# Reordering block 0 of a fused RWKV-6 and tanh-shrink kernel: decays ahead of the feed-forward part on VectorE in three steps, totals and first decays of block 1 in the boot, level 1 in step 0

## Chip, cores, metric

One core of one Trainium2 chip. The metric is the device time of one execution in microseconds (us). The program runs on one core only; the record gives the state of every run used here as fast. Runs of the kernel before still differ by up to 0.7% (those of one experiment by 1.1%), which matters for a change of this size; what the traces show of the reason stands at the end.

## The reference, cut

```python
# RWKV-6 attention, (batch, heads, seq, head_dim) = (4, 8, 768, 48)
for t in range(S):
    cur = np.einsum('bhd,bhe->bhde', u[None] * kt, vt)
    y[:, :, t] = np.einsum('bhd,bhde->bhe', rt, state + cur)
    state = wt[:, :, :, None] * state + np.einsum('bhd,bhe->bhde', kt, vt)
# then, on x = y as (3072, 384):
h = x @ w_in              # (384, 2048)
g = h - np.tanh(h)
return (g @ w_out).astype(np.float32)
```

Attention and feed-forward arithmetic are fp32; the two weight matrices arrive as 64-bit floats and are converted on the chip.

## The kernel before

The 3072 tokens are cut into 8 blocks of 384. Attention of a block is a doubling scheme over chunks of 64 tokens: at each level m = 1, 2, 4, 8, 16, 32 TensorE makes a gram matrix of r and k, VectorE or ScalarE copies the masked part of it out, and VectorE multiplies ("decays") half of k (`kq`) and half of r (`rp`) by products of w ("totals"), in place, for the next level. After that come a transpose ("turn"), the state update and the result.

Only block 0's attention runs alone, in the "boot". From then on, while the feed-forward part of block i runs in 16 steps f = 0 to 15, the attention of block i+1 is slotted between them. The listing sets the order on each engine, and no scheduler changes it later (`manual_schedule`). The trace shows VectorE keep to it: decay 2, listed behind the products of step 1, starts behind them at 60.40 us, though it could have begun at 56.7.

```python
def level(self, ps, m, p0, n, put_off=None):
    ...                                       # m == 32 has a variant of its own
    gr = self.gram(ps, self.tiles["kq"], self.tiles["rp"], p0, n, m, L // 2)   # TensorE
    ins = self.decay(m, p0, n)                # VectorE: kq, rp *= totals, after the gram has read them
    ...                                       # copies of the gram: VectorE for m <= 8, else ScalarE

def first(xT, f, ps):                         # feed-forward, step f
    hp = ps.tile([P, NB], F32, name="hp", tag="hp")
    for kc in reversed(range(KC)):            # 3 fp32 matmuls
        nc.tensor.matmul(hp, lhsT=w_in_sb[:, f, kc, :], rhs=xT[:, kc, :], ...)
    ...                                       # 6 activations on ScalarE: h, s, qa, qb, th, big
    return g, [ ... ], made                   # 5 products on VectorE, run later as "rest"

def plan(i):
    names = ("level 1", 2, 4, 8, 16, 32, "turn", "update", "result")
    if i == 0:
        steps = (1, 2, 3, 4, 6, 8, 10, 11, 13)                 # the step of each name
        before, behind = {0: ("totals 1", "kq", "rp")}, {1: ("totals 2",)}
        converted = (1, 3, 3, 4, 5, 7, 10, 10, 12, 13)         # steps of weight conversions 6 to 15
        loads = {f: "weights" for f in (1, 2, 3, 4, 6, 7, 8, 9, 10)}
    ...

for f in range(NF):                           # main loop of block i
    g, next_rest, made = first(here, f, ps_d)
    waiting.append((second, f, g))
    for n, op in enumerate(rest):             # products of step f - 1, mixed with the
        op()                                  # VectorE half of a weight conversion ("extra")
        if n >= 2 and extra:
            extra.pop(0)()
    for op in extra:
        op()
    rest = next_rest
    if later:
        for name in before.get(f, ()):
            later.prepare(name)               # totals, first decays
        if f in phases:
            later.phase(ps_a, phases[f])      # a level, turn, update or result of block i + 1
        ...
    for _ in range(converted.count(f)):
        extra += convert(*raws.pop(0))        # ScalarE half now, VectorE half in step f + 1
    if len(waiting) > LAG:                    # second matmul, three steps behind
        s, fs, gs = waiting.pop(0)
        s.add(fs, gs)
```

In what follows, hp5 is the first feed-forward matmul group of step 5, acc2 the second one of step 2 (TensorE runs it at the end of step 5), gram 8 the gram of level 8, decay 4 the pair of decays that level 4 makes, and gT the products' result that acc reads. In the traces each matmul of the listing shows as two, so a group of three is "x6".

## Time and profile before

| | before |
|---|---|
| median time, first three runs | 673.23 us (672.33 to 675.09) |
| span of the profiled run | 670.6 us |
| TensorE busy / granted clock over the span | 96% / 0.985 |
| VectorE, ScalarE busy | 81%, 73% |
| block 0 from hp0 to block 1's first hp | 84.6 us, of which 71.6 us is work at full clock |

"Busy" on TensorE says that an instruction was in flight, not that it ran at full clock (from 62.4 to 68.5 us it is busy for 6.10 of 6.10 us at a granted clock of 0.54), so busy share and granted clock are read together. The prediction shows the page, the stretches and TensorE's timeline. Its flips are changes of TensorE's granted clock between 0.50 and 1.00, its 952 is the time in ns of one decay (128x768, fp32), and its 400 is what the DMA engines moved, in GB/s (401 from 46 to 48 us, 412 from 48 to 50). What it tells in words only is the order on VectorE. This is VectorE's timeline of the kernel before (start, length, line, operation, output and inputs, shape), from the products of step 1 to decay 2:

```profile
56.72 0.55 DVE L488 SCALAR_TENSOR_TENSOR hs<-h,s 128x384 f32<-128x384 f32 x1
...
59.06 0.95 DVE L175 CUSTOM_DVE_ANT_0 w_sb<-w_sb,up 128x1536 uint16<-128x1536 uint16 x1
59.93 0.58 DVE L496 COPY_PREDICATED gT<-big,th 128x384 f32<-128x384 int32 x1
60.40 0.94 DVE L274 TENSOR_TENSOR kq<-kq,tot 128x768 f32<-128x768 f32 x1
61.27 0.95 DVE L274 TENSOR_TENSOR rp<-rp,tot 128x768 f32<-128x768 f32 x1
```

The two decays (the last two lines) could have begun at 56.7, when gram 2 had read what they overwrite, but 3.7 us of products and a conversion stand ahead of them. Gram 4 starts right after the last line has ended (62.36).

### The profile page before, as it was taken

The page shows a single profiled execution, that of the slowest core. Times are in us where ns is not written, and L with a number is a line of the kernel's source. Part 1 is how long each engine was busy: PE and PEld are TensorE (multiplying, and loading weights), DVE is VectorE, ACT ScalarE, POOL GpSimd, SP SyncE. Part 2 cuts the span into 40 slices and gives each one's busy share as a digit, 9 for nine tenths or more (in the row PEclk, how much of TensorE's full clock was granted, in tenths as well). Part 3 has the DMA queues.
Part 4 walks back from the last instruction along what each step waited for, and adds up shares of the span by engine and source line. Part 5 has one row for each costly group of instructions (what it writes and reads, how often), then busy time and mean ns, then how long its engine had stood idle before and what let it go on. Part 6 is the DMA issues. An engine that isn't in the chain of part 4 may idle for free.

```text
span 670.6 us, 19961 instructions
## 1 busy us (share of the span) xinstructions
PE 643.4 (96%) x8480; PEld 413.0 (62%) x8480; DVE 545.1 (81%) x1101; ACT 489.0 (73%) x966; POOL 5.0 (1%) x19
## 2 busy tenths in 40 slices
PE   4867999999999999999999999999999999999998
PEld 4745666566665666656665666656666566655554
DVE  7779998799778997599975998679976899746664
ACT  4678799775868667785776758677677857768785
POOL 2000000000000000000000000000000000000000
PEclk9968999999999999999999999999999999999999
DMA  8754354423112313121311231113131200000000
GB/s 316 224 209 149 103 177 137 151 72 97 50 55 58 112 49 96 58 70 50 96 49 57 72 95 51 52 53 120 50 95 38 91 3 2 2 11 35 1 0 36
DMA packets 30841, 54.37 MB, mean 81 GB/s; under 512 B 2336, under 2 KB 28704, under 8 KB 30752
## 3 DMA queue, kind: packets, MB, share of 16 engines
q1 hardware_dynamic: 30336, 52.80, 24.3%
q8 instruction: 67, 1.10, 0.7%
q10 hardware_dynamic: 352, 0.25, 0.1%
q14 instruction: 22, 0.18, 0.1%
q0 software_dynamic: 64, 0.05, 0.0%
HBM read 47.19 MB, written 4.72 MB: 77 GB/s over the span
## 4 chain that ended last, share of the span: by engine, by line
PE 76%; DVE 8%; issue 4%; PEld 4%; ACT 4%; DMA 2%; PEldq 1%; SPq 0%; DVEq 0%; ACTq 0%
PE acc L509 33%; PE hp L471 30%; PE att L242 8%; DVE states L371 2%; PE att L409 2%; PEld att L391 2%; PEld hp L471 2%; PE att L342 2%; PEld acc L509 1%; PE att L319 1%; DMA kq<-in_kT 1%; DVE rp L274 1%; DVE w_sb L175 1%; DVE hs L488 1%; DMA raw<-in_weights 1%
## 5 line engine op out<-in xcount | busy, mean ns | idle before, releaser
L471 PE MATMUL hp<-xT,w_sb 128*128 128x384 f32 x768 | 272.6, 492 | 3.0 <-ACT xT L423 2.1
L509 PE MATMUL acc<-w_sb,gT 128*128 128x384 f32 x768 | 275.2, 495 | 0.0
L471 PEld LDWEIGHTS hp<-xT,w_sb 128*128 128x128 f32 x768 | 147.2, 192 | 106.6 <-issue 2.4
L509 PEld LDWEIGHTS acc<-w_sb,gT 128*128 128x128 f32 x768 | 141.2, 191 | 89.5 <-ACT o L514 2.3
L478 ACT ACTIVATE h<-hp 128x384 f32<-128x384 f32 x128 | 62.9, 491 | 143.2 <-PE hp L471 142.5
L493 DVE TENSOR_TENSOR th<-h,th 128x384 f32<-128x384 f32 x128 | 70.9, 554 | 46.9 <-ACT th L482 46.8
L488 DVE SCALAR_TENSOR_TENSOR hs<-h,s 128x384 f32<-128x384 f32 x128 | 71.0, 554 | 27.2 <-ACT s L479 27.2
L496 DVE COPY_PREDICATED gT<-big,th 128x384 f32<-128x384 int32 x128 | 76.1, 595 | 12.8 <-ACT h L478 0.5
L480 ACT ACTIVATE qa<-s,shift 128x384 f32<-128x384 f32 x128 | 78.8, 615 | 4.2
L488 DVE SCALAR_TENSOR_TENSOR gT<-qb,hs 128x384 f32<-128x384 f32 x128 | 71.4, 558 | 9.2
L483 ACT ACTIVATE big<-s,shift 128x384 f32<-128x384 f32 x128 | 76.8, 600 | 0.0
L481 ACT ACTIVATE qb<-s,shift 128x384 f32<-128x384 f32 x128 | 76.8, 600 | 0.0
L488 DVE SCALAR_TENSOR_TENSOR hs<-qa,hs 128x384 f32<-128x384 f32 x128 | 70.5, 551 | 0.0
L479 ACT ACTIVATE s<-h 128x384 f32<-128x384 f32 x128 | 67.0, 523 | 4.0
L242 PEld LDWEIGHTS att<-rp,kq 48*64 48x64 f32 x3072 | 54.4, 148 | 22.5 <-issue 15.5
L482 ACT ACTIVATE th<-h 128x384 f32<-128x384 f32 x128 | 64.9, 507 | 0.0
L242 PE MATMUL att<-rp,kq 48*64 48x32 f32 x3072 | 58.3, 231 | 6.3 <-DVE rp L274 5.8
L274 DVE TENSOR_TENSOR kq<-kq,tot 128x768 f32<-128x768 f32 (+1 forms) x45 | 38.6, 857 | 2.8 <-PE att L319 1.6
L274 DVE TENSOR_TENSOR rp<-rp,tot 128x768 f32<-128x768 f32 (+1 forms) x45 | 38.8, 861 | 0.0
L371 DVE SCALAR_TENSOR_TENSOR states<-states,tot,att 128x48 f32<-128x48 f32 x176 | 31.5, 256 | 8.9 <-PE att L360 8.9
L302 DVE COPY_PREDICATED scores<-mask_all,att 128x384 f32<-128x384 uint8 (+1 forms) x54 | 31.8, 654 | 0.0
L242 PE MATMUL att<-rmix,kmix 48*64 48x64 f32 x768 | 14.5, 232 | 6.8 <-ACT rmix L222 6.8
(54 smaller groups left out, 336.4 us busy)
## 6 DMA issues: line engine op xcount, KB each, us to landing
raw<-in_weights SPq DMA_DIRECT2D x16, 768.0 KB, 4.4
rmix<-in_rT SPq DMA_DIRECT2D x7, 768.0 KB, 4.8
kmix<-in_kT SPq DMA_DIRECT2D x7, 768.0 KB, 4.8
wt<-in_wT SPq DMA_DIRECT2D x7, 768.0 KB, 4.7
kq<-in_kT SPq DMA_DIRECT2D x7, 768.0 KB, 5.2
rp<-in_rT SPq DMA_DIRECT2D x7, 768.0 KB, 4.6
v_sb<-in_v SPq DMA_DIRECT2D x8, 576.0 KB, 4.2
out_y<-o SPq DMA_DIRECT2D x23, 192.0 KB, 1.9
```

What stands on the lines that cost most here:

```text
L242: nc.tensor.matmul(dst, lhsT=lhs[rows, t0:t0 + L], rhs=src, start=True, stop=True)
L274: ins = nc.vector.tensor_tensor(out=part, in0=part, in1=by, op=ALU.mult)
L471: nc.tensor.matmul(hp, lhsT=w_in_sb[:, f, kc, :], rhs=xT[:, kc, :], start=(kc == KC - 1), stop=(kc == 0))
L479: nc.scalar.activation(out=s, in_=h, func=AF.Square)
L480: nc.scalar.activation(out=qa, in_=s, func=AF.Square, bias=shift[:, 0:1])
L481: nc.scalar.activation(out=qb, in_=s, func=AF.Square, bias=shift[:, 1:2])
L482: nc.scalar.activation(out=th, in_=h, func=AF.Tanh)
L483: nc.scalar.activation(out=big, in_=s, func=AF.Relu, bias=shift[:, 2:3])
L488: return lambda: nc.vector.scalar_tensor_tensor(out=out, in0=in0, scalar=scalar, in1=in1, op0=op0, op1=ALU.mult)
L493: lambda: nc.vector.tensor_tensor(out=th, in0=h, in1=th, op=ALU.subtract),
L496: lambda: nc.vector.copy_predicated(out=g, mask=big.bitcast(I32), data=th)], made
L509: nc.tensor.matmul(acc, lhsT=g[:, j * P:(j + 1) * P], rhs=w_out_sb[:, f, :], start=(f == 0), stop=(f == NF - 1))
```

## The change

The intent is to keep TensorE fed in block 0. It has four parts: work moved into the boot; earlier steps for each level; in steps 4 to 6 ("urgent") the level's VectorE work listed ahead of the products; and, not named in the title, later steps for most weight conversions.

```diff
         if i == 0:
-            steps = (1, 2, 3, 4, 6, 8, 10, 11, 13)
-            before, behind = {0: ("totals 1", "kq", "rp")}, {1: ("totals 2",)}
-            converted = (1, 3, 3, 4, 5, 7, 10, 10, 12, 13)
-            loads = {f: "weights" for f in (1, 2, 3, 4, 6, 7, 8, 9, 10)}
+            steps = (0, 2, 4, 5, 6, 7, 9, 10, 12)
+            before, behind, urgent = {}, {}, (4, 5, 6)
+            converted = (3, 4, 5, 5, 7, 9, 9, 10, 11, 13)
+            loads = {f: "weights" for f in (0, 1, 2, 3, 4, 6, 7, 8, 9, 10)}
 ...
@@ boot, after the loads of kq and rp
-        more_weights(nc.sync)
-        for _ in range(2):
-            ready.append(convert(*raws.pop(0)))
         while ready:
             converted()
+        for name in ("totals 1", "totals 2"):
+            later.prepare(name)
+        for name in ("kq", "rp"):
+            ready.append(convert(*raws.pop(0)))
+            converted()
+            later.prepare(name)
 ...
@@ main loop; finish() runs the products and conversions, as before
-            (products and conversions)
+            if f not in urgent:
+                finish(rest, extra)
             if later:
                 (prepare, phase)
+            if f in urgent:
+                finish(rest, extra)
```

More of the change, by code (lines that the diff above doesn't have):

```diff
@@ L530, in plan @@
             before = {0: ("kmix",), 1: ("rmix",), 2: ("totals 1",), 3: ("totals 2", "kq"), 4: ("rp",)}
-            behind, converted = {}, ()
+            behind, converted, urgent = {}, (), ()
             loads = {2: "v", 5: "rmix", 7: "kmix", 9: "wt", 11: "kq", 14: "rp"}
-        return dict(zip(steps, names)), before, behind, converted, loads
+        return dict(zip(steps, names)), before, behind, converted, loads, urgent
     blocks = [Block(b, q) for b in range(B) for q in range(NQ)]
@@ L625, with finish @@
     waiting, rest, extra = [], [], []
+    def finish(rest, extra):
+        for n, op in enumerate(rest):
+            op()
+            if n >= 2 and extra:
+                extra.pop(0)()
+        for op in extra:
+            op()
     for i, blk in enumerate(blocks):
@@ L631 @@
             xT = later.begin()
-        phases, before, behind, converted, loads = plan(i)
+        phases, before, behind, converted, loads, urgent = plan(i)
         second = Second(blk.b * S + blk.q * NB, ps_d)
@@ L636 @@
             waiting.append((second, f, g))
-            for n, op in enumerate(rest):
-                op()
-                if n >= 2 and extra:
-                    extra.pop(0)()
-            for op in extra:
-                op()
-            rest = next_rest
+            if f not in urgent:
+                finish(rest, extra)
             if later:
@@ L651 @@
                     later.prepare(name)
+            if f in urgent:
+                finish(rest, extra)
+            rest = next_rest
             name, ins = loads.get(f), None
```

## The prediction

> **What bounds the kernel now.** I read the page first (busy shares and the slices), then the engines in long stretches, then TensorE and VectorE in order of time through block 0, then the DMA landings. The page:
>
> ```profile
> PE 643.4 (96%) x8480; PEld 413.0 (62%) x8480; DVE 545.1 (81%) x1101; ACT 489.0 (73%) x966; POOL 5.0 (1%) x19
> ...
> PE   4867999999999999999999999999999999999998
> ...
> PEclk9968999999999999999999999999999999999999
> ```
>
> TensorE is full from the fifth slice to the end; a change of order can only win in the first four (to about 67 us) or in what they hand on. The stretches of block 0, from its first feed-forward matmul (42.5) to the first of block 1 (127.1):
>
> ```profile
> 42.50:51.00 8.50, 7.53 (x11) 3.71 (x12) 5.90 (x8) 6.44 (x10) 0.00 (x0) 0.50 0.93 359
> 51.00:58.90 7.90, 7.89 (x206) 5.09 (x204) 7.66 (x17) 7.24 (x14) 0.00 (x0) 1.00 0.45 139
> 58.90:62.40 3.50, 0.04 (x4) 0.07 (x5) 3.50 (x6) 3.44 (x8) 0.00 (x0) 0.83 0.80 274
> 62.40:68.50 6.10, 6.10 (x102) 4.62 (x103) 5.96 (x10) 3.07 (x4) 0.00 (x0) 0.54 0.14 55
> 68.50:97.00 28.50, 28.50 (x363) 17.70 (x362) 28.09 (x51) 24.96 (x47) 0.00 (x0) 1.00 0.40 134
> 97.00:127.10 30.10, 29.19 (x355) 18.89 (x354) 24.70 (x60) 27.73 (x52) 0.00 (x0) 1.00 0.41 128
> ```
>
> Columns: length, busy PE, PEld, DVE, ACT, POOL, granted clock, DMA share, GB/s. TensorE idles 3.5 us while VectorE is full, and then works at half clock. Who ended that wait is in TensorE's timeline:
>
> ```profile
> 42.54 4.21 PE L471 MATMUL hp<-xT,w_sb 128*128 128x384 f32 x6 [2.07 <-ACT xT L423]
> 47.68 3.81 PE L471 MATMUL hp<-xT,w_sb 128*128 128x384 f32 x6 [0.93 <-ACT h L478]
> ...
> 62.36 2.79 PE L242 MATMUL att<-rp,kq 48*64 48x32 f32 x96 [3.47 <-DVE rp L274]
> 65.08 3.65 PE L509 MATMUL acc<-w_sb,gT 128*128 128x384 f32 x6
> 68.56 2.10 PE L471 MATMUL hp<-xT,w_sb 128*128 128x384 f32 x6
> ```
>
> The gram of level 4 waits for VectorE's level-2 decay of rp. Six full-rate matmuls take 1.94 us (the spacing late in the chain); here 4.21, 3.81 and 3.65. Work between 42.54 and 127.14: 29 groups of six (hp 0 to 15, acc 0 to 12) x 1.94 = 56.3, plus attention 1.6 (level 1) + 4 x 1.55 + 1.0 + 1.4 + 1.6 + 3.5 = 15.3; sum 71.6. It takes 84.6. So 13 us are lost, all but 1 of them before 68.5, and not 3.5 as the wait alone suggests.
>
> [...]from two-microsecond stretches I place the flips at 51.0 (up), 61.2 (down) and 68.0 (up), 10.2 and 6.8 us apart[...]; gaps under 1 us later flip nothing. [...]a decay waits behind the feed-forward products listed before it. So listing order is priority, which is what this change edits. [...]the trace has 952 here, spaced 0.87. Moving a decay makes it no cheaper. [...]the trace has about 400 at 46 to 50 us[...].
>
> **The change, part by part.**
>
> *Boot.* VectorE waits 1.86 and 1.16 us there for weight conversions (ends of idle at 43.44 and 46.35). The six totals (0.98 + 0.48 + 1.03 = 2.5 us of spacing) go into that idle time: free. The two level-1 decays (1.73) cannot: kq was issued at 41.48 and took 6.0 us (47.5), rp at 42.11 took 7.5 (49.6). Dropping the seventh weight load[...] should land rp about 0.7 earlier (estimate: 2.36 MB instead of 2.7 MB moved by then). On VectorE: totals 41.5 to 44.0, conversion of weights 4 to 45.6, decay kq 47.5 to 48.4, conversion 5 to 49.9, decay rp to 50.8. Today these decays end at 51.2: only 0.4 us won, plus 1.0 of totals out of the later path.
>
> *Level 1 in step 0.* TensorE runs hp0 to 46.75 and then the level-1 gram instead of waiting 0.93 for ScalarE. It should be at full clock by 51.0 as now[...].
>
> *Rest of block 0.* I replayed the three queues in the new order with durations from this trace: hp or acc 1.94; gram 1.6; ScalarE's six activations 3.0, a conversion there 1.6; on VectorE, five products 2.65 alone, 3.7 with one conversion, 5.2 with two; a pair of decays 1.73; copies 1.81 (level 1), 1.67 (level 2), 0.93 (levels 4, 8); state updates 3.55. A gram reads what the next decay overwrites, so a decay also waits for its own step's gram. VectorE: level-1 copies 50.8 to 52.6, products of step 0 to 55.25, of step 1 to 57.95, decays and copies of level 2 to 61.35, products of step 2 to 64.0. Then, decays first: level 4 to 66.8, products 3 with conversion 6 to 70.5, level 8 to 73.1, products 4 with conversion 7 to 76.8, decay 16 to 78.5, products 5 with conversions 8 and 9 to 83.75, products 6 and decay 32 to 88.2, and so on to the states at 103.3.
>
> TensorE against it: hp4 starts at 60.4 (now 68.56), 8.2 us won, with no idle stretch longer than about 1.5 us[...]. But from there it is held by VectorE: hp6 wants weights 6 (69.9), gram 16 wants decay 8 (72.2), hp8 wants weights 8 (81.7), and hp9, hp10 and hp11 start at 86.1, 91.5 and 97.3 instead of back to back, for ScalarE's activation, conversion 10 and conversion 11. The result starts at 103.4 (now 113.08), one step earlier in the order, and hp of block 1 at about 121.3, now 127.14. So 8.2 won and 2.4 given back: **5.8 us**. A cross-check: VectorE's waits in block 0 today sum to about 8 us (3.5 up to 47 us, 2.5 at 97 to 104, 2 after 119); the new order uses most of them. All later blocks have a full TensorE, so the gain is kept to the end: 673.2 - 5.8 = 667.4. A replay forgets small waits, so I put back about half a microsecond: **668.0 us**, 0.8% faster.
>
> **Rivals.**
>
> *A, the whole loss comes back.* If VectorE kept up, only the cold first group (2.3 us) and the drain in the result would stay: 71.6 + 3 instead of 84.6, 10 us, 663. For it: TensorE's idle time and clock are what shows. Against it: VectorE is 28.09 busy of 28.50 from 68.5 to 97, and its work is moved, not cut. This is also the floor, so 2% (13.5 us) is out of reach.
>
> *B, the urgent decays make new waits.* In steps 4 to 6 VectorE now stands still until that step's gram is done, where it had worked through five products meanwhile; and the products, ready later, hold back acc three steps on. Also later conversions (6 at step 3, 7 at 4) bring weights close to their use. For it: my replay has VectorE finishing level 4 just after the gram, with no slack, and weights 6 within a microsecond of hp6. Against it: three steps between gT and acc are some 15 us here, and only weights, not gT, come out late. It would leave 1 to 3 us of gain: 670 to 672.
>
> *C, the boot is hidden anyway or gets worse.* The rp decay waits for its landing whatever the order, now ahead of the level-1 copy in a strict queue; if kq or rp landed 2 us later, everything behind moves by as much, and the gain falls to about 4: 669.5. [...]Against it: one load fewer in that queue.
>
> **Range and chances.** My replay gives 667.4, A 663, B 670 to 672, C 669.5. The three times before span 672.3 to 675.1, so the median itself may move by a microsecond. The range 664.5 to 671.5 takes in B's better half and all but the end of A. Faster by over 2% needs more than the floor allows: 2%. Slower by over 2% would need a new wait of over 13 us or a repeated fall of the clock: 2%. Within 2%: 96%.
>
> **What would show it right or wrong.** Right: level-1 decays end near 50.8 and the totals lie before 45; TensorE has no 3.5 us gap near 59 and a granted clock of 1.0 from about 51 on; VectorE is over 95% busy from 51 to 100; hp4 starts near 60; the first matmul of block 1 near 121; everything after it is shifted by the same amount. A is right if that matmul comes by 117.5; B if VectorE shows waits on PE att at levels 4 and 8, or hp on weights, over 3 us in all; C if the kq or rp decay ends after 52. I am wrong at the root if the time after block 0 changes by more than a microsecond, or if the clock falls once more in block 0.

## The result and the profile after

Ratios here are the mean time of one kernel's fast runs over that of the other's in the same rounds, so not quite the ratio of the medians quoted.

| | before | after |
|---|---|---|
| median (range), 4 runs each | 673.62 us (672.33 to 675.09) | 667.73 us (667.57 to 668.64) |
| ratio, 95% interval | | 0.9915 [0.9892, 0.9938] |
| the same, measured again (chip 13), 35 and 6 runs | 672.35 us | 667.38 us, 0.9917 [0.9900, 0.9935] |
| span of the profiled run | 670.6 us | 665.8 us |
| boot, up to hp0 | 42.54 us | 43.31 us |
| block 0, hp0 to block 1's hp | 84.60 us | 79.48 us |
| everything after | 543.5 us | 543.0 us |

667.73 us was measured against 668.0 predicted, inside the range. Less than 1%, so "within 2%". The span shows where it came from: block 0 is 5.1 us shorter, the rest stays within half a microsecond (over all profiled runs of this document it lies between 542.1 and 544.0), and the boot was 0.8 us longer in that run (a difference of runs: in the second profiled run of the changed kernel hp0 starts at 42.11; see the end).

The page of the kernel after; busy times, TensorE's slices and its clock:

```profile
PE 642.6 (97%) x8480; PEld 412.0 (62%) x8480; DVE 545.2 (82%) x1101; ACT 488.7 (73%) x966; POOL 4.6 (1%) x19
...
PE   5879999999999999999999999999999999999997
...
PEclk9959999999999999999999999999999999999999
```

The work is the same (x8480, x1101, x966, busy times within 1 us); the fourth slice of TensorE went from 7 to 9, and three others moved by one. On its clock the page shows almost nothing; a slice of 17 us is too coarse. The same stretches as in the prediction, for the kernel after:

```profile
42.50:51.00 8.50, 7.69 (x106) 4.94 (x107) 6.32 (x12) 7.17 (x12) 0.00 (x0) 0.61 0.98 335
51.00:58.90 7.90, 7.32 (x114) 4.39 (x114) 7.62 (x14) 6.46 (x13) 0.00 (x0) 1.00 0.67 231
58.90:62.40 3.50, 3.50 (x25) 1.90 (x25) 3.50 (x5) 3.44 (x8) 0.00 (x0) 1.00 0.73 211
62.40:68.50 6.10, 6.10 (x156) 4.19 (x151) 5.96 (x12) 5.89 (x11) 0.00 (x0) 1.00 0.42 151
68.50:97.00 28.50, 28.18 (x412) 17.48 (x405) 28.02 (x50) 27.79 (x50) 0.00 (x0) 1.00 0.41 134
```

In the third line TensorE is busy for 3.50 of 3.50 us where it was 0.04, and in the fourth its clock (third number from the end) is 1.00 where it was 0.54. The last line holds the price: TensorE is now at 28.18 instead of 28.50, and both VectorE (28.02) and ScalarE (27.79, before 24.96) are nearly full.

That the clock has its part is seen in the timed runs too. The record gives each run's mean granted clock over the whole span: 0.980 to 0.987 in the 98 runs of the kernel before that were made beside the experiments, 0.989 to 0.992 in all ten of the changed one. TensorE's timeline of the kernel after:

```profile
43.31 4.21 PE L471 MATMUL hp<-xT,w_sb 128*128 128x384 f32 x6 [2.07 <-ACT xT L423]
47.45 2.37 PE L242 MATMUL att<-rmix,kmix 48*64 48x64 f32 x96
...
60.17 2.10 PE L471 MATMUL hp<-xT,w_sb 128*128 128x384 f32 x6
62.20 1.60 PE L242 MATMUL att<-rp,kq 48*64 48x32 f32 x96
...
98.69 2.17 PE L471 MATMUL hp<-xT,w_sb 128*128 128x384 f32 x6 [0.58 <-DVE w_sb L175]
```

Level 1 follows hp0 without a gap, hp4 starts at 60.17, gram 4 follows it without a wait, and hp11 waits 0.58 us for its weights from VectorE. VectorE's timeline after, around decays 2 and 4:

```profile
58.63 0.94 DVE L274 TENSOR_TENSOR kq<-kq,tot 128x768 f32<-128x768 f32 x1
59.49 0.95 DVE L274 TENSOR_TENSOR rp<-rp,tot 128x768 f32<-128x768 f32 x1
...
64.75 0.94 DVE L274 TENSOR_TENSOR kq<-kq,tot 128x768 f32<-128x768 f32 x1
65.61 0.94 DVE L274 TENSOR_TENSOR rp<-rp,tot 128x768 f32<-128x768 f32 x1
```

Decay 2 is done 1.8 us before gram 4 asks for it, decay 4 1.2 us before gram 8 does (67.79).

### The profile page after: what moved, and what is told of

Its sections match the earlier page's. It is cut to its first block, busy times and chain, and to the rows that moved or that the text cites. A ratio compares the mean times of both kernels' runs of the same rounds, so it can differ in the third digit from the quotient of the medians.

```text
span 665.8 us, 19964 instructions
## 1 busy us (share of the span) xinstructions
PE 642.6 (97%) x8480; PEld 412.0 (62%) x8480; DVE 545.2 (82%) x1101; ACT 488.7 (73%) x966; POOL 4.6 (1%) x19
## 4 chain that ended last, share of the span: by engine, by line
PE 80%; DVE 5%; issue 4%; PEld 4%; ACT 4%; DMA 1%; PEldq 1%; SPq 0%; DVEq 0%
PE acc L509 33%; PE hp L471 32%; PE att L242 9%; PE att L409 2%; DVE states L371 2%; PEld hp L471 2%; PEld att L391 2%; PE att L342 2%; PEld acc L509 1%; PE att L319 1%; DMA wt<-in_wT 1%; DVE rp L274 1%; DVE w_sb L175 1%; ACT scores L330 1%; PEldq L397 1%
## 5 line engine op out<-in xcount | busy, mean ns | idle before, releaser
L493 DVE TENSOR_TENSOR th<-h,th 128x384 f32<-128x384 f32 x128 | 71.0, 555 | 46.1 <-ACT th L482 46.0
L480 ACT ACTIVATE qa<-s,shift 128x384 f32<-128x384 f32 x128 | 78.8, 615 | 4.2
```

Source lines behind the costliest of these rows:

```text
L480: nc.scalar.activation(out=qa, in_=s, func=AF.Square, bias=shift[:, 0:1])
L493: lambda: nc.vector.tensor_tensor(out=th, in0=h, in1=th, op=ALU.subtract),
```

## The experiments

The theory: TensorE's loss in block 0 is one wait for a decay that stands behind other work in VectorE's queue, made about twice as dear by the clock that falls in it (0.54 on average from 62.4 to 68.5 us); the order on VectorE and the idle time of the boot together remove it, and then VectorE's own pace sets what is won. Rivals: the boot or the earlier steps carry the gain alone; the clock is a bystander; TensorE's cold start (hp0 takes 4.21 us at a clock of 0.50) is what limits the changed kernel.

All results in one table. "Gain" is (1 - ratio) x 672.4 us; "block 0" is the time from hp0 to block 1's first hp in the profiled run. It leaves out the scatter of hp0's start, but not wholly: in the two profiled runs of the changed kernel hp0 starts at 43.31 and 42.11 and block 1 at 122.79 and 122.87, so one reads 79.5 and the other 80.8. Each ratio is against the kernel before on the same chip (22 to 41 runs of it; three chips in all). All outputs were correct.

| kernel | median us (runs) | ratio [95%] | gain us | block 0 us |
|---|---|---|---|---|
| before | 672.4 (41) | 1 | 0 | 84.6 |
| changed, again | 667.38 (6) | 0.9917 [0.9900, 0.9935] | 5.6 | 80.8 (first run 79.5) |
| changed, order put back | 672.11 (14) | 0.9995 [0.9979, 1.0010] | 0.3 | 84.0 |
| before, order alone | 669.87 (12) | 0.9964 [0.9950, 0.9979] | 2.4 | 81.0 |
| changed, boot put back | 669.48 (6) | 0.9958 [0.9941, 0.9975] | 2.8 | 80.9 |
| before, boot alone | 670.95 (22) | 0.9976 [0.9962, 0.9991] | 1.6 | 84.0 |
| changed, conversions put back | 671.12 (22) | 0.9974 [0.9964, 0.9985] | 1.7 | 82.3 |
| changed, level 1 in step 1 | 667.55 (6) | 0.9922 [0.9904, 0.9940] | 5.2 | 79.4 |
| before, ten matmuls in the gap | 673.47 (14) | 1.0016 [0.9999, 1.0033] | -1.1 | 84.9 |
| before, five matmuls in the gap | 670.35 (17) | 0.9968 [0.9957, 0.9980] | 2.2 | 82.6 |
| changed, kq and rp loaded first | 667.75 (6) | 0.9918 [0.9898, 0.9937] | 5.5 | 79.5 |
| changed, warm start | 667.25 (6) | 0.9918 [0.9898, 0.9937] | 5.5 | 79.7 |
| changed, both of these | 666.97 (6) | 0.9920 [0.9897, 0.9944] | 5.4 | 78.5 |

The second measurement of the changed kernel was expected at 0.9915 with less scatter than the kernel before has: it came at 0.9917, with a standard deviation of 0.7 us against 1.2.

### The order put back

```diff
-            before, behind, urgent = {}, {}, (4, 5, 6)
+            before, behind, urgent = {}, {}, ()
```

> The changed kernel with the order in steps 4 to 6 put back: the feed-forward products and conversions first, the decays behind them. Theory (priority on VectorE is what counts): replayed with the changed trace's durations, decays 4, 8 and 16 end some 3.7, 4 and 5 us later, the grams of levels 8, 16 and 32 wait for them by about 2.4, 0.8 and 2.4 us, part of which comes out of waits the changed kernel has later; 2 to 3 us slower than the changed kernel, so 669.7 to 670.7. Rival (the earlier steps and the boot did it, the order is neutral): within 0.5 us of 667.7.

It lost nearly everything: 0.9995. The edit moves nothing but the products and VectorE's half of the conversions in steps 4 to 6, all on VectorE. TensorE's timeline shows why it lost more than I expected (the profiled run is one of the slower of the 14, 674.5 us, with hp0 only at 46.05):

```profile
67.46 2.10 PE L471 MATMUL hp<-xT,w_sb 128*128 128x384 f32 x6
73.09 2.55 PE L242 MATMUL att<-rp,kq 48*64 48x32 f32 x96 [3.53 <-DVE rp L274]
75.57 4.21 PE L509 MATMUL acc<-w_sb,gT 128*128 128x384 f32 x6
```

The wait of the kernel before is back at the same length, 3.53 us, one level later (gram 8), and behind it six matmuls take 4.21 us. I had expected 2.4 us there. And its stretches (two microseconds each; the third number from the end is the clock):

```profile
72.00:74.00 2.00, 0.91 (x45) 0.94 (x47) 2.00 (x5) 2.00 (x4) 0.00 (x0) 0.85 0.70 259
74.00:76.00 2.00, 2.00 (x64) 1.94 (x59) 2.00 (x5) 1.94 (x3) 0.00 (x0) 0.50 0.03 8
```

The clock is at half from about 73.4 on. So the earlier steps, the boot and the new conversion times together are worth 0.3 us (-0.7 to 1.4) without the order.

### The order alone

```diff
from the kernel before: its boot, steps, conversions and loads; of the change only the main loop, with
-            before, behind = {0: ("totals 1", "kq", "rp")}, {1: ("totals 2",)}
+            before, behind, urgent = {0: ("totals 1", "kq", "rp")}, {1: ("totals 2",)}, (2, 3, 4, 6)
```

> The kernel before with nothing but the order changed: in steps 2, 3, 4 and 6, which hold levels 2, 4, 8 and 16 there, the decays go ahead of the products; boot, steps, conversions and loads as before. Theory: the gram of level 4 no longer waits 3.5 us (decay 2 ends near 58.5 instead of 62.2), the clock does not fall, and the result starts near 108.5 instead of 113.1: about 4.5 us faster than before, 669. Rival (boot and steps carry the gain): no more than 1 us faster, 672.5 or above.

0.9964: 2.4 us, about half of what I expected, and clearly more than the rival's 1. Gram 4 did start without a wait, but the profiled run has another wait one level earlier (TensorE's timeline):

```profile
55.56 1.72 PE L242 MATMUL att<-rp,kq 48*64 48x32 f32 x96 [2.20 <-DVE scores L249]
57.21 3.72 PE L471 MATMUL hp<-xT,w_sb 128*128 128x384 f32 x6
```

Gram 2 waited 2.20 us for VectorE to copy level 1 out (it stands behind the first decays and products there, and the gram needs the buffer), and the clock fell at about 56.9, so hp3 took 3.72 us. I had overlooked that wait in the replay. The new order does not make it, as up to there VectorE's list is that of the kernel before. It shows where the clock has risen early (hp1 takes 2.20 us here and 3.81 in the profiled run of before), and 0.73 us of it is a late landing of rp. All five profiled kernels with level 1 in step 1 and an early clock have it (1.01 to 2.20 us, with the old boot and with the new), and none with level 1 in step 0. So the order alone leaves a stall that comes with the early clock; how much of the missing 2 us it makes, one trace cannot tell.

### The boot put back, and the boot alone

```diff
 boot_undone, from the changed kernel: boot tail and loads as before, and
+            before, behind, urgent = {0: ("totals 1", "kq", "rp")}, {1: ("totals 2",)}, (4, 5, 6)
 boot_only, from the kernel before: boot tail and loads of the change, before = behind = {}
```

> The changed kernel with only the boot put back: totals and first decays of block 1 are in steps 0 and 1 again, and the seventh weight load is in the boot. Theory: VectorE is about 1.4 us later from the products of step 1 on (1.0 of totals, 0.4 of decays) and is what later steps wait for, so 1 to 1.5 us slower than the changed kernel, 669. Rival (the boot is hidden, as the decays wait for their loads whatever the order): within 0.4 us of 667.7. Rival (the boot is the main part): 671 or more.

> The kernel before with only the boot changed (and the seventh weight load moved from boot to step 0): steps, order and conversions as before. Theory: decay 2 ends 1.4 us earlier, so the wait of the gram of level 4 shrinks from 3.5 to about 2 us; whether the clock falls in that gap[...]. 1.4 us faster than before if it falls all the same, up to 4 if it doesn't: 669.6 to 672.2, and more scatter between runs than the changed kernel has. Rival (hidden): 673 or above.

Boot put back: 0.9958, 2.8 us less gain than the changed kernel (2.1 by the medians), against 1 to 1.5 expected: the direction is right, and the two intervals together leave some 1.6 us either way, so the size cannot be told from mine. TensorE's list of waits in block 0 of that kernel (who, for whom: us in total, times, longest):

```profile
PE hp L471 <- DVE w_sb L175: 1.6, 4, 0.6
PE att L242 <- DVE rp L274: 1.0, 2, 0.6
```

The changed kernel has none of the second kind; of the first it has 0.8 us in two waits in its first profiled run and 1.6 in four in its second. Decay 2 ends 18.5 us after hp0 with the boot put back, and 17.1 and 18.5 after it in the two runs of the changed kernel. So the traces show VectorE late, and not how much of that the boot makes. Boot alone: 0.9976, in the expected range, and with the widest scatter of all (667.4 to 674.9; standard deviation 1.9 us against 0.6 for the changed kernel). Its profiled run had the gram-4 wait at 2.65 us and a fallen clock; its fastest runs are as fast as the changed kernel. The mean clocks of its runs bear out that the clock falls in some and not in others: the five runs at 0.981 and 0.982 take 672.8 us on average, the four at 0.989 and 0.990 take 668.2.

### Conversions put back

```diff
-            converted = (3, 4, 5, 5, 7, 9, 9, 10, 11, 13)
+            converted = (1, 3, 3, 4, 5, 7, 10, 10, 12, 13)
```

> The changed kernel with the weight conversions at the steps where they were before (1, 3, 3, 4, 5, 7, 10, 10, 12, 13). Theory (the new times take work off VectorE before the decays of levels 2 to 8): decay 2 ends 1 us later, grams 16 and 32 wait 2 and 1 us, and weights 12, converted in step 10 behind the state updates, hold hp12 by over 2 us: 2 to 2.7 us slower than the changed kernel. Rival (conversions are only moved about): within 0.5 us of it.

0.9974, so 3.9 us of the gain gone (3.7 by the medians), more than the 2 to 2.7 expected. The waits are where the replay put them (TensorE's timeline):

```profile
75.14 1.60 PE L242 MATMUL att<-rp,kq 48*64 48x32 f32 x96 [2.04 <-DVE rp L274]
...
81.49 1.01 PE L319 MATMUL att<-rp,kq 48*32 48x32 f32 x96 [0.68 <-DVE rp L274]
...
105.45 2.17 PE L471 MATMUL hp<-xT,w_sb 128*128 128x384 f32 x6 [2.28 <-DVE w_sb L175]
```

Gram 16 by 2.04, gram 32 by 0.68 and hp12 by 2.28 us. In this run the clock fell neither in the 2.04 nor in the 2.28 us gap. The mean clocks of the timed runs divide the loss: the 13 runs at 0.989 or above, as high as the changed kernel's, take 670.6 us on average, 3.1 more than the changed kernel's 667.4, and the 9 at 0.986 or 0.987 take 672.2. So most of the loss comes without a fall of the clock, and falls in part of the runs add some 0.7 us to the mean.

### Level 1 in step 1

```diff
-            steps = (0, 2, 4, 5, 6, 7, 9, 10, 12)
+            steps = (1, 2, 4, 5, 6, 7, 9, 10, 12)
```

> The changed kernel with level 1 in step 1, where it was. Theory: VectorE has the same work before decay 2, so its times hardly move; TensorE waits 0.7 to 0.9 us for ScalarE after hp0 again: 0 to 0.7 us slower than the changed kernel. Rival (level 1 in step 0 is a main part, by the cold start it covers): 1.5 us or more slower.

0.9922 against 0.9917: no difference that 6 runs can show. TensorE again waits 0.91 us for ScalarE after hp0 and 1.09 us before gram 2, and gives nothing away by it: block 0 is 79.4 us. Level 1 in step 0 is not where the gain is, though six runs against six leave room for a microsecond (difference of the means 0.3, give or take 1.0).

### What the fall of the clock costs

In the kernel before, matmuls without use fill TensorE's wait ahead of gram 4; they write to an accumulator that is overwritten afterwards.

```diff
             g, next_rest, made = first(here, f, ps_d)
+            if i == 0 and f == 3:
+                second.open()                  # allocates the accumulators early
+                for _ in range(10):            # second kernel: range(5)
+                    nc.tensor.matmul(second.acc[0], lhsT=w_in_sb[:, 0, 0, :], rhs=here[:, 0, :],
+                                     start=True, stop=True)
```

> The kernel before with ten idle-time matmuls (about 3.2 us, results overwritten) ahead of the gram of level 4, where TensorE stands still for 3.5 us; nothing else differs and the wait itself stays. Theory (the fall of the clock doubles what the wait costs): no fall near 61 us, gram 1.6 and six products 1.94 instead of 2.8 and 3.65, 2.3 us faster than before: 0.9966. Rival (VectorE alone sets the pace, the clock is a bystander): no more than 0.5 us.

> As the run with ten matmuls in the gap, which were twice too long ([...]6.5 us in its trace instead of 3.2, so the gram came 3 us later than before and took the gain back); now five, about 3.2 us. Theory (the fall of the clock costs some 2.6 us on top of the wait): 2 to 2.6 us faster than before, 0.996 to 0.997. Rival: within 0.5 us of it.

Ten were a mistake of mine: each is two instructions in the trace, so they took 6.5 us and not 3.2. The slip shows the cost of the clock best (TensorE's timeline):

```profile
58.88 6.61 PE L642 MATMUL acc<-xT,w_sb 128*128 128x384 f32 x20
65.42 1.60 PE L242 MATMUL att<-rp,kq 48*64 48x32 f32 x96
66.95 2.20 PE L512 MATMUL acc<-w_sb,gT 128*128 128x384 f32 x6
68.99 2.10 PE L471 MATMUL hp<-xT,w_sb 128*128 128x384 f32 x6
```

Counted from hp0 (42.93 here, 42.54 before), gram 4 starts at 22.5 instead of 19.8 us, 2.7 us later than before; yet hp4 starts at 26.1 against 26.0. The gram and acc0 at full clock (1.60 and 2.20, before 2.79 and 3.65) make up the 2.7 us. So the fall of the clock costs 2.6 us beside the wait of 3.5, in these two runs and up to hp4. The kernel with ten gains nothing by it, as the later gram takes it back (84.9 against 84.6 us in block 0; -1.1 us in the timed runs, -2.2 to 0.1). With five matmuls the kernel gained 2.2 us (0.9968), as expected and against the rival's half microsecond. One reservation: in the profiled run of that kernel the clock had fallen earlier, at about 57.4, behind a wait of 1.38 us, so that trace does not show a clock that never falls; and in 11 of its 17 timed runs the mean clock is 0.986 or 0.987, no higher than in the best runs of before. The time of the 17 runs and the trace of the run with ten carry the point.

### What holds the changed kernel back

```diff
 kq_first, from the changed kernel:
-        begin_behind(ins, more_weights(nc.sync))
-        later.load("kq", kT, 0, NPAIR)
+        begin_behind(ins, later.load("kq", kT, 0, NPAIR))
         later.load("rp", rT, 0, NPAIR)
+        more_weights(nc.sync)
   and conversion 5 out of the boot:
-            converted = (3, 4, 5, 5, 7, 9, 9, 10, 11, 13)
+            converted = (2, 3, 4, 5, 5, 7, 8, 9, 10, 11, 13)
 warm_start, from the changed kernel, ahead of hp0:
+        spare = scratch(ps)
+        for _ in range(2):
+            nc.tensor.matmul(spare[:, 0, 0:256], lhsT=w_in_sb[:, 0, 0, :], rhs=w_sb[:, 0, 0:256],
+                             start=True, stop=True)
 both: the two together
```

> The changed kernel with the boot's last loads in the order kq, rp, weights 5 instead of weights 5, kq, rp; conversion 5 goes from the boot to step 2 and conversion 11 from step 9 to step 8. Theory (VectorE is what hands out the waits that are left): its 1.7 us wait for kq goes, first decays end near 49 instead of 51.5, and the 0.6 us wait of hp11 for its weights goes: 1 to 1.7 us faster than the changed kernel, 0.989 to 0.990 of before. Rival (TensorE's cold start sets the pace now): no change, 0.9917.

> The changed kernel with two idle-time matmuls ([...]about 1.8 us cold, into a spare tile) where TensorE waits 2.1 us ahead of hp0[...]. If the clock then rises before or in hp0, hp0 and the level-1 gram take 1 to 3 us less. Theory (VectorE sets the pace): 0 to 1 us faster than the changed kernel, 0.990 to 0.9917. Rival (the cold start sets it): 1.5 to 3 us.

> The last two edits together on the changed kernel. Theory: each frees what holds the other, so more than their sum: 2 to 3 us faster than the changed kernel, 664.5 to 665.5, 0.9875 to 0.9890 of before. Rival: the sum of the two alone.

None of the three is distinguishable from the changed kernel: 0.9918, 0.9918 and 0.9920, on another chip than its 0.9917. Each did at first what it was meant to do. With kq and rp first, the decay of rp starts at 49.14 instead of 50.64 and VectorE reaches decay 2 1.5 us sooner; then hp9 waits for ScalarE, behind conversion 11 that I had moved to step 8, and the state update for ScalarE's copies (TensorE's timeline):

```profile
87.41 2.20 PE L471 MATMUL hp<-xT,w_sb 128*128 128x384 f32 x6 [1.13 <-ACT h L478]
...
95.37 1.61 PE L360 MATMUL att<-v_sb,ks 64*64 64x48 f32 x80 [0.57 <-ACT ks L344]
```

With the warm start, the two spare matmuls take 2.07 us, the clock rises at about 45.5 us instead of 49.1, hp0 takes 3.05 instead of 4.21 us and the level-1 gram 1.63 instead of 2.37; the time comes back as waits for VectorE's conversions:

```profile
43.73 3.05 PE L471 MATMUL hp<-xT,w_sb 128*128 128x384 f32 x6
...
71.14 2.17 PE L471 MATMUL hp<-xT,w_sb 128*128 128x384 f32 x6 [0.38 <-DVE w_sb L175]
...
77.50 2.18 PE L471 MATMUL hp<-xT,w_sb 128*128 128x384 f32 x6 [0.41 <-DVE w_sb L175]
```

The second profiled run of the changed kernel has waits of 0.41 us before hp6 and hp7 too, without a warm start. Its hp0 came 1.2 us earlier than in the first run, while rp landed late on VectorE (its timeline):

```profile
50.77 0.96 DVE L274 TENSOR_TENSOR rp<-rp,wt 128x768 f32<-128x768 f32 x1 [1.05 <-DMA rp<-in_rT]
```

Block 1 then starts at 122.87 us as against 122.79. TensorE ahead of VectorE, by an edit or by chance, is held by it within 35 us. So the rival "cold start" is not borne out: its 1.5 to 3 us are not seen, though the intervals leave some 1.8 us either way. My hope of 2 to 3 us from both together is not seen either. The shortest block 0, 78.5 us, is that kernel's, but its times (665.5 to 670.1) do not show a gain, so no version here is called better than the changed kernel.

## Why the prediction was right, step by step

**What bounds, and the size of the loss.** Right. 13 us were lost in block 0; the changed kernel loses 7.9 (79.48 - 71.6). The prediction's claim that the wait of 3.5 us costs more than itself was shown by the filled gap: 2.6 us more.

**The boot.** From hp0 on, the replay put the end of the first decays at 50.8 - 42.54 = 8.3 us; the trace has 51.59 - 43.31 = 8.3 (the second profiled run 9.6, as hp0 comes earlier and the decays end at 51.73). The totals went into idle time (42.2 to 44.9). One term was wrong: dropping the seventh load was to land rp 0.7 us earlier; it took 7.3 us instead of 7.5. It cost nothing in that run, as VectorE came to that decay only at 50.64, behind kq and a conversion. In the second run rp took 9.1 us and VectorE waited 1.05 for it; over all profiled runs with this order of loads it took 7.3 to 9.1 us (median 7.4) without the seventh load in the boot and 7.5 to 8.9 (median 7.6) with it, so a gain of 0.7 is not seen. The prediction counted the boot at 1.4 us of VectorE's time; taking it back costs 2.8 us in the timed runs, give or take 1.6, which agrees.

**Level 1 in step 0.** The prediction gave it no number of its own in the sum; moving it back changes nothing measurable.

**The replay.** hp4 was to start 17.9 us after hp0 and did so after 16.9, so 9.2 us were won there and not 8.2: the clock rose 5.8 us after hp0 and not 8.4 (at about 49.1 and 51.0), where the replay had left it as it was. The state updates end 60.8 us after hp0 in the replay and in the trace. The result starts 61.4 against 60.9, block 1's hp 79.5 against 78.8. So 4.1 us were given back and not 2.4, and the net is 5.1 in the trace and 5.6 in the times against 5.8. That the net comes so close is in part luck, as the two errors have opposite signs; in the second profiled run it is 3.8. That the extra microsecond at hp4 was gone by the state updates is the point of the prediction in small: behind step 5 VectorE sets the pace, and TensorE's lead is only lent. The waits appeared where named (hp10 0.16, hp11 0.58), not all of the named size: at hp6 and gram 16 the first profiled run has none (the second 0.41 at hp6).

**The rivals.** A (all 10 us come back, 663) is out: VectorE is 47.97 of 49.0 us busy from 51 to 100, and starting TensorE earlier is given back. B (urgent decays make new waits) is out: VectorE has no wait for a gram in steps 4 to 6, and TensorE's waits on VectorE in block 0 sum to 0.8 us (1.6 in the second run) against the 3 set as the mark. C (loads land late) is out by its mark, a decay that ends after 52: 51.59 and 51.73. But in the second run a late rp did hold VectorE for 1.05 us.

**What the prediction did not say** is how the parts hang together. Alone, the order is worth 2.4 us and the boot 1.6; all but the order is worth 0.3, all but the boot 2.8, all but the conversion times 1.7, all together 5.6. They do not add up. The traces suggest why: with a part left out, TensorE waits in another place (gram 8 without the order; grams 16 and 32 and hp12 without the conversion times; grams 4 and 8 without the boot), and some of these waits take the clock down with them. This is read from one trace each, not tested by itself. The conversion times, which the title does not name, are needed too: leaving them out costs 3.9 us, the order 5.3.

**Left open.** How much of the gain that the order alone lacks is the wait of gram 2; whether level 1 in step 0 is worth a few tenths. The earlier steps of the levels from 4 on were never put back alone, and the conversion times never tried alone.

## What to carry to other kernels

Where an engine works in the order of the listing, as VectorE does here (decay 2 starts 3.7 us after it could have), list first what another engine will wait for next, and let the work with slack (here products wanted three steps later) stand behind it; check that every engine that feeds the bottleneck can keep up, or the gain is only lent (here VectorE is busy for 47.97 of 49.0 us). Price a wait of TensorE with what may follow it at a lower clock (here 2.6 us more behind a wait of 3.5), not with its own length alone. And judge the parts of such a reordering by leaving one out as well as by adding one alone: here the order and the boot, 2.4 and 1.6 us alone, cost 5.3 and 2.8 when left out, and the conversion times 3.9.

## What else the traces show

- The length of TensorE's gap did not tell by itself whether the clock falls: it fell behind gaps of 3.47 us (before), 2.20 us (order alone) and 1.38 us (five matmuls in the gap), and stayed up in others of 2.28 and 2.04 us (conversions put back) and 1.37 us (ten matmuls). The fall cost 2.6 us, as much as half of what the change won.
- Three 128x384 fp32 matmuls take 1.94 us at full clock, and the profile shows each as two instructions of 0.32 us; counting them as one made a filler of mine twice too long.
- TensorE has waits marked "issue" in the boot, ahead of the first results, that no trace here explains: 1.5 us in the runs of before and after first profiled, 2.4 in the order-alone and boot-put-back runs, 3.2 with the order put back. With the clock that falls near there at different moments (34.9 to 37.3 us in these runs), hp0 starts anywhere from 42.1 to 46.1 us in kernels whose code up to there has the same order, which may be much of the scatter between runs (670.5 to 675.1 us for the kernel before on one chip); only the profiled runs show hp0.
